# Recurrent attention and a squared-ReLU layer on one core: decays by TensorE, one written list for the first two groups, two more pieces in passes

## The chip, the cores and the metric

The kernel runs on 1 core of one Trainium2 chip. The metric is the device time of the program in microseconds (us). A core has engines that each work through their own instructions in order: TensorE (PE; its weight loads are shown as PEld), VectorE (DVE), ScalarE (ACT), GpSimd (POOL) and SyncE (SP), whose queue here issues all transfers. They wait for each other through semaphores. On-chip data lies in SBUF; TensorE writes into the eight banks of PSUM.

## The reference

Two blocks, one after the other. First a gated recurrence over 768 steps for 4 batches and 8 heads of width 48; then a layer with 2048 hidden units on the 3072 rows of 384 numbers that come out. All data of q, k, v and alpha are float32; `w_in` and `w_out` come as float64.

```python
for t in range(S):
    state = alpha[:, :, t, :, None] * state + np.einsum('bhd,bhe->bhde', k[:, :, t], v[:, :, t])
    y[:, :, t] = np.einsum('bhd,bhde->bhe', q[:, :, t], state)
...
x = attn_out.transpose(0, 2, 1, 3).reshape(B * S, H * D)
h = np.maximum(x @ w_in, 0.0)
return (h * h @ w_out)
```

## The kernel before

**Blocks.** The 768 steps are cut into 6 chunks of 128 and with 4 batches make 24 blocks of 128 rows, numbered chunk by chunk (block n is chunk n // 4 of batch n % 4). For a block, ScalarE takes logarithms of alpha (`ln`, L244), TensorE sums them along the steps with a triangular matrix (`cs`, L265 for blocks 0 to 7 in fp32, L268 and L269 after that in two parts), and ScalarE takes exponentials of the sums and of their negatives (`eb` L276, `ei` L280). VectorE multiplies q by the one and k by the other (`mq`, `mk`, L284). TensorE transposes q and k (`qT`, `kT`, L309 for blocks 0 to 3; `turn`, L482, after that, for pairs of blocks) and ScalarE or VectorE copies them out of PSUM (`qc`, `kc`, L325 and L490). Then come scores within half-blocks (`scores`, L372) and the sums of k times v (`state_sums`, L395), a masked copy of the scores (`masked`, L380), and the state: `sums_copied` (L406) and `next_state` (L420 and L421), which multiplies the new state by the decay over the whole block. Two blocks of one pair share the y products (`ga` and `gb`, L352), and `ev` (L515) copies y in twelve pieces into x, which is laid out feature by row.

**The decay over a block** is the last row of the exponentials. `bl` (L297) writes this row to DRAM, and `br` (L303) reads it back twice, element by element, so that it lies along partitions in `last`. Both go through SP's queue.

**Groups.** Four blocks, 512 rows, make a group; there are six. The layer runs group by group: 16 hidden units of 128 columns each (`ffn_in` or `in_x` with `in_y`), and then the output, four tiles of 128 rows by 384 columns, each the sum over the 16 hidden units. `w_in` and `w_out` are each cut into eight pieces of two hidden units (768 KB as float64). A piece is loaded (`load_weights`) and turned into float32 by five VectorE and two ScalarE instructions (`convert_first` L153 and L157, `convert_middle` L166 and L169, `convert_second` L175, L179, L182).

**Two kinds of products.** A plain product is fp32 (L806 for the hidden units of group one, `out_plain` for some pieces of the output). The other kind runs in three passes in the faster fp32r type: each operand is split into a high part, a rest and their difference (for w: `cast_w` L551, `rest_w` L561, `diff_w` L571; for x and the hidden values: `split_to` L597 and L598, `diff_to` L547), and three products are added (L623 for hidden units, L702 for the output, both `in_x`/`in_y` and `out_x`/`out_y`). The parts of w are also written to DRAM and read back for later groups (`keep` L556, `pump` L590). Group one uses plain products for all hidden units and for six pieces of `w_out`, and passes for the last two pieces. Group two uses passes for its hidden units, plain products for four pieces of `w_out` and passes for four (`AT['k0'] = 2`, `AT['k1'] = 4`). Groups three to six use passes throughout.

**The order of the work.** Nothing is scheduled by a compiler: each engine's order is the order in which the program calls the steps. For the first blocks it is a list of words in the code:

```python
first = """
    ln0 cs0 ei0 mk0 warm0 eb0 bl0 mq0 kT0 load0v kc0 ln1 qT0 load2a load2k cs1
    ...
    load4a kv3 am3 us3 load4k middle1 ha1 second1 ya2 yb2 ev2 weights4 first2
    ha0 hb1 middle2 hb0 st2 st3 st1
"""
```

`warm` and `zeros` in it are products whose result nobody uses (L221 and L338; `zeros` has three, on a state that holds zeros). After the list, `weave` walks through the units of TensorE's work of a group (`layer_in`, `layer_out`), adds up their costs, and puts in attention steps, conversions and splits of w when the sum reaches the time set for each (`AT`, `PLAN`, `EARLY`). A buffer that is used again makes its next writer wait for its last reader; the two alpha tiles serve blocks n % 2 (blocks 2 and 3 borrow others), and raw weight pieces have four buffers.

## Time and profile before

| | |
|---|---|
| device time, median of 3 runs | 521.2 us (520.43 to 521.31) |
| span of the profiled execution, the time of it that the page gives | 518.9 us |
| TensorE busy | 509.3 us, 98%, 5276 products |
| VectorE busy | 368.7 us, 71% |
| ScalarE busy | 299.6 us, 58% |
| transfers | 102.35 MB, mean 197 GB/s |
| chain that ended last | 93% on PE: o L702 41%, h L623 32%, h L806 7% |
| plain output products, L702 o<-w_out,hid | 160 records, 53.5 us |
| plain hidden products, L806 | 108 records, 43.7 us |
| copies of y, L515 on ACT | 132, 46.9 us |

An fp32 product shows as two records, one in passes as one for each pass. The page cuts the span into 40 slices of 13 us and shows the busy share of each engine in tenths, the clock granted to TensorE and the share of the transfer engines. Busy times are unions: overlapping instructions are not counted twice, so the mean duration of one instruction can be longer than its share of the busy time.

### The profile page before, as it was taken

The numbers are of one execution on the slowest core, as the hardware profiler recorded it, in microseconds if no ns is written. First come the engines' busy times: TensorE is split into PE (matmuls) and PEld (weight loads), VectorE is DVE, ScalarE is ACT, GpSimd is POOL, SyncE is SP. The second block draws the span as 40 slices with busy tenths as digits, with TensorE's granted clock in tenths as the row PEclk, the third lists the DMA queues.
The fourth block names the chain that finished last, engine by engine and source line by source line (L and its number), as shares of the span: only waits on it lengthen the run. The fifth ranks groups of instructions, "written<-read, shape, count | busy, mean of one in ns | idle before, by whom it ended". The sixth has DMA issues, their size and how long they took to land.

```text
span 518.9 us, 12889 instructions
## 1 busy us (share of the span) xinstructions
PE 509.3 (98%) x5276; PEld 417.9 (81%) x5276; DVE 368.7 (71%) x635; ACT 299.6 (58%) x630; POOL 5.3 (1%) x29
## 2 busy tenths in 40 slices
PE   7989999999999999999999999999999999999997
PEld 4854455668887669988899988899988899988997
DVE  4798979977978788875795576695465585364861
ACT  4668785666758554575954275954275754154620
POOL 4000000000000000000000000000000000000000
PEclk9999999999999999999999999999999999999999
DMA  9999767451879586999966787866773545898201
GB/s 160 211 267 215 206 216 239 105 170 72 265 174 223 121 303 171 290 315 209 270 145 172 257 247 193 245 156 165 241 245 124 186 120 153 273 340 294 67 0 62
DMA packets 140995, 102.35 MB, mean 197 GB/s; under 512 B 111477, under 2 KB 114569, under 8 KB 140937
## 3 DMA queue, kind: packets, MB, share of 16 engines
q1 hardware_dynamic: 140936, 101.53, 69.1%
q8 instruction: 42, 0.69, 0.5%
q14 instruction: 17, 0.13, 0.1%
HBM read 84.18 MB, written 17.33 MB: 196 GB/s over the span
## 4 chain that ended last, share of the span: by engine, by line
PE 93%; DMA 4%; DVE 1%; SPq 1%; ACT 1%; issue 0%; DVEq 0%
PE o L702 41%; PE h L623 32%; PE h L806 7%; PE y L352 4%; PE T L482 2%; PE sckv L372 2%; PE sckv L395 2%; DMA a_in<-in_alpha_dram 1%; DMA a_lent<-in_alpha_dram 1%; DMA k_in<-in_k_dram 1%; PE cs L265 1%; DMA row<-b 1%; PE cs L269 1%; DVE x L515 1%; PE cs L268 1%; SPq L109 0%
## 5 line engine op out<-in xcount | busy, mean ns | idle before, releaser
L623 PE MATMUL h<-xa,wb 128*128 128x512 f32 x240 | 68.4, 393 | 0.0
L623 PE MATMUL h<-xl,wl 128*128 128x512 f32 x240 | 67.7, 390 | 0.0
L638 ACT ACTIVATE hid<-h 128x512 f32<-128x512 f32 x40 | 23.8, 598 | 74.8 <-PE h L623 74.7
L623 PE MATMUL h<-xd,wd 128*128 128x512 f32 x240 | 66.8, 393 | 0.0
L515 ACT COPY x<-y 32x256 f32<-32x256 f32 (+2 forms) x132 | 46.9, 366 | 30.0 <-PE y L352 24.8
L702 PE MATMUL o<-wb,ha 128*128 128x384 f32 x160 | 54.5, 341 | 0.0
L702 PE MATMUL o<-wd,hd 128*128 128x384 f32 x304 | 53.7, 334 | 0.0
L702 PE MATMUL o<-w_out,hid 128*128 128x384 f32 x160 | 53.5, 490 | 0.0
L702 PE MATMUL o<-wl,hl 128*128 128x384 f32 x160 | 53.5, 335 | 0.0
L623 PEld LDWEIGHTS h<-xl,wl 128*128 128x128 f32 x240 | 45.1, 188 | 9.7
L702 PEld LDWEIGHTS o<-wd,hd 128*128 128x128 f32 x304 | 52.8, 188 | 0.0
L623 PEld LDWEIGHTS h<-xa,wb 128*128 128x128 f32 x240 | 44.5, 188 | 9.3
L623 PEld LDWEIGHTS h<-xd,wd 128*128 128x128 f32 x240 | 44.4, 188 | 9.0
L702 PE MATMUL o<-wb,hx 128*128 128x384 f32 x144 | 49.0, 340 | 0.0
L702 PE MATMUL o<-wl,hx 128*128 128x384 f32 x144 | 48.2, 334 | 0.0
L702 PEld LDWEIGHTS o<-w_out,hid 128*128 128x128 f32 x160 | 29.9, 190 | 19.7
L806 PE MATMUL h<-x,w_in 128*128 128x512 f32 (+1 forms) x108 | 43.7, 553 | 1.2 <-ACT x L515 1.2
L547 DVE TENSOR_TENSOR hid<-h,hid 128x512 f32<-128x512 f32 x40 | 27.5, 688 | 23.4 <-PE h L623 23.3
L806 PEld LDWEIGHTS h<-x,w_in 128*128 128x128 f32 x108 | 19.9, 190 | 20.9 <-issue 17.0
L597 ACT ACTIVATE ha<-hid 128x512 fp32r<-128x512 f32 x40 | 25.2, 638 | 17.2 <-DVE hl L598 10.8
L640 ACT ACTIVATE h<-h 128x512 f32<-128x512 f32 x40 | 23.3, 583 | 17.1 <-PE h L623 14.1
L547 DVE TENSOR_TENSOR osb<-o,osb 128x384 f32<-128x384 f32 x24 | 12.9, 553 | 25.8 <-PE o L702 24.6
(113 smaller groups left out, 879.5 us busy)
## 6 DMA issues: line engine op xcount, KB each, us to landing
wd<-do SPq DMA_DIRECT2D x36, 384.0 KB
wl<-lo SPq DMA_DIRECT2D x34, 384.0 KB
wl<-li SPq DMA_DIRECT2D x32, 384.0 KB
wd<-di SPq DMA_DIRECT2D x32, 384.0 KB
raw<-in_moe_w_in_dram SPq DMA_DIRECT2D x8, 768.0 KB
raw<-in_moe_w_out_dram SPq DMA_DIRECT2D x8, 768.0 KB
v_in<-in_v_dram SPq DMA_DIRECT2D x24, 192.0 KB
out_dram<-osb SPq DMA_DIRECT2D x24, 192.0 KB
```

The source lines that it names most:

```text
L352: ins = nc.tensor.matmul(out=ys[e][64 * half : 64 * half + D + G * e, m % 2, p // 2, t], lhsT=lhsT, rhs=rhs, start=(half, e) not in seen, ...
L372: nc.tensor.matmul(out=ps[e][HALF[h], 0, p, :], lhsT=ks[rows, p, HALF[h]], rhs=qs[rows, p, HALF[h]], start=True, stop=True, skip_group_che ...
L395: nc.tensor.matmul(out=ps[h][64 * e : 64 * (e + 1), 1, p, G:64], lhsT=tile_of("k", n)[HALF[h], 2 * p + e, :], rhs=tiles["v"][n % NV][HALF[ ...
L482: nc.tensor.transpose(out=ps[h][:, i, p, :], in_=rows[HALF[h], 128 * p : 128 * (p + 1)], identity=ident[HALF[h], HALF[h]],)
L515: copy(out=x[kk][to : to + m, t : t + 2], in_=blk[n]["y"][e][r : r + m, :, p // 2],)
L547: nc.vector.tensor_tensor(out=o, in0=x, in1=z, op=op)
L597: nc.scalar.activation(out=a, in_=x, func=AF.Copy, scale=NEAR * E)
L623: nc.tensor.matmul(out=acc["h", j], lhsT=here[w, "i", p][:, kk, jj * 128 : (jj + 1) * 128], rhs=x_parts[x][:, kk], start=start and kk == 0 ...
L638: nc.scalar.activation(out=hid[j], in_=x, func=AF.Copy, scale=E)
L640: nc.scalar.activation(out=x, in_=x, func=AF.Copy, scale=1.0 + E)
L702: nc.tensor.matmul(out=acc[t][:, 0:DM], lhsT=lhs[:, t * C : (t + 1) * C], rhs=rhs, start=start, stop=stop, skip_group_check=True,)
L806: nc.tensor.matmul(out=ps, lhsT=w[:, kk, c0 : c0 + 128], rhs=xT[g][kk][:, cols], start=(kk == 0), stop=(kk == KM - 1),)
```

## The change

**Decays by TensorE.** For blocks 0 to 3 the row no longer goes through DRAM. The step `dl` multiplies the logarithms with the last column of the triangular matrix, eight products of one column each, so that the sums over the block come out along partitions; `de` takes their exponentials into `last`, in two ScalarE instructions. Blocks from 4 on keep `bl` and `br`.

**One list for groups one and two.** The word list now covers everything up to the last product of group two, some 900 words, and the planner is used for groups three to six alone. The steps are finer: conversions to DRAM (`kept_l`, `kept_d`), fetches back (`fetch`), the ScalarE and VectorE halves of a split (`split_h` and `rest_h`, `split_x` and `rest_x`), each copy of y (`moved`), each half of a masked copy, transposes block by block (`turned_one`), the ReLU and the square after a hidden unit, and the scaling and adding behind products are words of their own. The hidden units of group one run in another order, and the loads of the weight pieces stand earlier in the list.

**Six pieces of group two.** Group two has plain products for two pieces of `w_out` and passes for six (`out_plain:p:t:2` and `out_x:n:t:4`). The number of plain pieces in group one stays six.

**No zero products.** The words `zeros` are gone from the order; four `warm` products remain, two at the start. All copies of y and of the transposed q and k go to ScalarE; twelve copies of y and two of the transposes were VectorE's.

```diff
-AT = {..., 'k0': 2, 'h0': 15, 'k1': 4, 'h1': 3, 'h1by': 5, ...}
+ORDER = """
+load:3:a load:0:a ln:0 warm:0 warm:0 cs:0 eb:0 ei:0 load:1:a ln:1 warm:0 load:0:k load:0:q mq:0 cs:1 ln:3 cs:3
+ei:3 eb:3 dl:3 eb:1 mk:0 ei:1 qT:0 dl:1 de:1 load:1:k mk:1 qc:0 load:1:q mq:1 qT:1 qc:1 load:2:a ln:2 kT:1
+load:3:q mq:3 kT:0 cs:2 qT:3 kc:1 load:3:k mk:3 load:1:v eb:2 ei:2 load:2:q mq:2 load:0:v sc:1 kv:1 kc:0 sc:0
+de:3 qc:3 one_masked:1:1 one_masked:1:0 us:1 kv:0 one_masked:0:0 one_masked:0:1 kT:3 kc:3 load_weights:0 dl:0
+de:0 us:0 qT:2 qc:2 sa:0 first:0 middle:0 y_states:0 y_inner:0 yb:0 moved:0:0:0 dl:2 de:2 load:2:k mk:2
+load:4:a kT:2 kc:2 warm:0 load:3:v sc:3 second:0 ln:4 kv:3 one_masked:3:0 load:2:v one_masked:3:1 us:3 sc:2
+kv:2 one_masked:2:0 moved:0:0:1 moved:0:0:2 moved:0:1:0 moved:0:1:1 moved:0:1:2 moved:0:2:0 load_weights:1
+moved:0:2:1 moved:0:2:2 moved:0:3:0 moved:0:3:1 moved:0:3:2 load:5:a cs:4 ha:1 one_masked:2:1 us:2 sa:2 eb:4
+y_states:2 first:1 load_weights:2 load_weights:3 sa:3 middle:1 y_inner:2 yb:2 ln:5 second:1 first:2 load:4:k
+moved:2:0:0 load_weights:4 moved:2:0:1 bl:4 load_weights:5 moved:2:0:2 moved:2:1:0 load:6:v moved:2:1:1
+moved:2:1:2 moved:2:2:0 moved:2:2:1 moved:2:2:2 ha:0 load:7:v moved:2:3:0 moved:2:3:1 moved:2:3:2 ei:4
+load:5:q first:3 middle:3 second:3 cs:5 eb:5 hf:2 middle:2 second:2 rf:2 ra:1 load:4:q load_weights:6 qa:1
...
+"""
...
-    for _ in range(3):
-        warm(0)
...
+    def dl(n):
+        ps = blk[n]["cs"].rearrange("a p t -> a (p t)")
+        for p in range(NP):
+            for e in range(2):
+                first = (2 * p + e) * D
+                nc.tensor.matmul(
+                    out=ps[64 * e : 64 * e + D, H * D + p : H * D + p + 1],
+                    lhsT=blk[n]["logs"][:, first : first + D], rhs=causal[:, C - 1 : C],
+                    start=True, stop=True, skip_group_check=True,
+                )
+
+    def de(n):
+        ps = blk[n]["cs"].rearrange("a p t -> a (p t)")
+        for e in range(2):
+            rows = slice(64 * e, 64 * e + D)
+            nc.scalar.activation(out=last_t[n % 4][rows], in_=ps[rows, H * D : H * D + NP], func=AF.Exp)
...
-    VECTOR = ('k0', 'q0')
+    VECTOR = AT["vec"].split()
...
-            if w == "i" or p >= NW - AT["k0"] or (x == "l" and p >= NW - AT["k1"]):
+            if w == "i" or p >= NW - 2 or (x == "l" and p >= NW - 6):
                 here[x, w, p] = t
...
+    def fetch(*key):
+        here[key] = wt("w" + key[0], FP32R, shapes[key[1]])
+        nc.sync.dma_start(out=words(here[key]), in_=kept_parts[key])
...
-    first = """
-        ln0 cs0 ei0 mk0 warm0 eb0 bl0 mq0 kT0 load0v kc0 ln1 qT0 load2a load2k cs1
...
+    for word in ORDER.split():
+        f, *given = word.split(":")
+        steps[f](*(int(x) if x.isdigit() else x for x in given))
...
-    for g in range(1, NG):
+    for g in range(2, NG):
```

More of the change, by code (lines that the diff above doesn't have):

```diff
@@ L341, in zeros @@
             )
-    SHARED = (0, 2)
     def y_begin(n):
@@ L462, in gb, with y_first, y_states @@
[L462 to L472 removed]
+    def y_first(a):
+        y_states(a)
+        y_inner(a)
+    def y_states(a):
+        product = two["y"] = y_begin(a)
+        for h in range(1 if a < B else 0, 2):
+            for m, p, e in heads(a):
+                rows = slice(64 * e, 64 * e + D)
+                s = blk[m]["u" if h else "s"]
+                product(m, p, e, s[rows, p, G * (1 - e) : 64], blk[m]["qs"][rows, p, HALF[h]], HALF[h])
@@ L499, in ev, with moved @@
+    def moved(n, p, i):
         g, t = divmod(n, GB)
-        if t == 0 and ps[0] == 0:
+        if g not in xT:
             if g == 0:
```

511 lines of the change are left out of this document (267 added, 244 removed).

## The prediction

> **What bounds the kernel now.** I read the page's slices first, then TensorE's waits, the windows by stage, the timeline of the head, and last the chain of waits.
>
> ```profile
> PE   7989999999999999999999999999999999999997
> PEclk9999999999999999999999999999999999999999
> DMA  9999767451879586999966787866773545898201
> ```
>
> TensorE is full from the third slice (13 us each) to the last, at full granted clock. The eight waits listed for it sum to 5.8 us, all before 36 us; the longest:
>
> ```profile
> PE kT L309 <- DVE k_in L284: 1.3, 1, 1.3
> PE h L806 <- ACT x L515: 1.2, 3, 0.7
> ...
> PE sckv L395 <- DMA v_in<-in_v_dram: 1.0, 2, 0.8
> ```
>
> The windows (length; busy of PE, PEld, DVE, ACT, POOL; clock; DMA share; GB/s) give what else is full:
>
> ```profile
> 0.00:13.00 13.00, 9.15 (x94) 5.89 (x94) 6.19 (x12) 5.46 (x10) 5.34 (x29) 1.00 0.99 160
> ...
> 26.00:36.00 10.00, 8.12 (x171) 5.79 (x163) 9.77 (x21) 5.33 (x12) 0.00 (x0) 1.00 1.03 246
> 36.00:52.00 16.00, 16.00 (x42) 7.80 (x42) 13.44 (x23) 14.32 (x27) 0.00 (x0) 1.00 0.98 238
> 52.00:80.00 28.00, 28.00 (x219) 13.74 (x218) 24.66 (x40) 23.11 (x42) 0.00 (x0) 1.00 0.73 211
> 80.00:127.40 47.40, 47.40 (x561) 33.12 (x560) 40.89 (x65) 30.61 (x62) 0.00 (x0) 1.00 0.48 148
> ```
>
> So the kernel has two parts: a head of 36 us, set by transfers and copies, and TensorE without a hole. Time is won by less TensorE work or by filling TensorE earlier, and lost by any new hole. From the timeline (start, length, what; in brackets the idle time before and what ended it):
>
> ```profile
> 1.10 2.93 PE L221 MATMUL warm<-s 128*128 128x256 f32 x6 [1.10 <-POOL s L67]
> ...
> 3.73 0.52 ACT L244 ACTIVATE a_in<-a_in 128x384 f32<-128x384 f32 x1 [1.72 <-DMA a_in<-in_alpha_dram]
> ...
> 16.65 0.52 ACT L244 ACTIVATE a_lent<-a_lent 128x384 f32<-128x384 f32 x1 [2.64 <-DMA a_lent<-in_alpha_dram]
> ...
> 19.63 4.05 PE L338 MATMUL zeros<-s 128*128 128x256 f32 x18
> ...
> 26.52 0.68 PE L395 MATMUL sckv<-v_in,qk_lent 64*64 64x48 f32 x32 [0.20 <-DMA v_in<-in_v_dram]
> ```
>
> The first input tile lands at 3.73, the twelfth at 16.65: 1.175 us each. The sixteenth (26.52) has two weight pieces ahead of it: (26.52 - 3.73 - 15 x 1.175) / 2 = 2.6 us a piece, decay rows included. The chain (start, length, what):
>
> ```profile
> 35.28 9.72 PE h L806 x26
> ...
> 175.56 13.10 PE o L702 x40
> ...
> 207.19 8.54 PE o L702 x48
> ...
> 515.45 0.56 DVE osb L547
> ```
>
> From 35.28 TensorE works 480.2 us to 515.45; 3.45 us of tail follow.
>
> **Six pieces in passes.** An fp32 product is two records: 40 records in 13.10 us, 0.655 us a product. Three passes: 3 x 0.175 (a run of 144 takes 25.18 us) = 0.525. Pieces 2 and 3 of group two hold 16 products: 16 x 0.13 = -2.1 us, all on the path. Added: four splits, on VectorE 4 x (0.685 + 0.692) = 5.5 us and on ScalarE 4 x 0.63 = 2.5, and two fetches of 384 KB, 1.9 us each at 206 GB/s. VectorE is busy 75.1 of the 88.3 us of group two and DMA some 0.75, so these cost nothing; uncovered, 5.5 us. The order mixes fp32 with passes: 33 changes between the kinds, 4 before. The nearest row, four passes of a sum of logs inside an fp32 run, shows none (12 records and 8 passes in 5.26 us after it, 5.33 by their rates); the other end is 18 passes after transposes, 4.33 against 4.12 after such sums: 29 x 0.2 = 6 us. I take 0. Returns from small attention products to large ones fall from 33 to 28: up to -1.0.
>
> **Zero products.** Twelve go, 5.6 us of busy time before 24 us, where TensorE waits anyway: 0, unless they keep its clock (first rival).
>
> **Decays of blocks 0 to 3.** Four row stores and eight gathers leave SP's queue; one store is on the chain at 23.61 (3.87 us). Added per block: eight one-column products, between 0.25 us (16 records at the 16 ns of the y products) and 0.65 (a whole sum of logs); I take 0.6, in a waiting TensorE; and two ScalarE exponentials, 0.25 each, below the smallest copy's 0.367. New wait: block 4's alpha reuses block 0's tile and must wait for block 0's decay products, and v of blocks 3 and 2 and w_in piece 1 stand behind it on SP. Tile 13 (v of block 0) lands at 3.73 + 12 x 1.175 = 17.8; state sums, k's transposes of block 3 and the decays take 1.5, so SP goes on at 19.3, while piece 0 and one k are still in flight to 21.6: nothing lost.
>
> **The head's new order.** ScalarE now makes all 24 copies of y (12 were VectorE's) and becomes its path. Piece 0 is behind 13 tiles: 3.73 + 12 x 1.175 + 2.6 = 20.4. Then VectorE's first step 0.48, ScalarE's two steps of piece 0 1.65, one copy 0.385 (six of them, start to next, 2.28 us; three 1.17), decay 0.5, k copy 0.48, logs 0.42, 11 copies 4.24, exponential 0.37, piece 1 1.65, logs 0.42, 12 copies 4.62: 15.2 in all, so x of group one is whole at 35.6, against 35.28 before. But TensorE has done other things by then. Before, four half-width products (0.43) and all 42 full ones (0.87) were left. Now six and 40 are left, and the sums of logs of blocks 4 and 5 (0.65 each) are done: 480.2 + 0.86 - 1.74 - 1.3 - 2.1 = 475.9.
>
> **New holes in groups one and two.** From x whole to the first product in passes, TensorE's list holds 0.87 + 13 x 2.62 full columns, 2.6 halves, 3.5 transposes, 4.3 scores and sums, 4.1 logs, 4.1 y and 17 x 1.31 out = 75.8 us. VectorE ends piece 3's conversion 3.9 us after that point (0.37 + 0.84 on ScalarE, then 2.73) and then has 12 x 2.73 + 11 x 0.94 (conversions), 6 x 0.87 (splits of w), 12 x 0.47 (q and k), 12.2 (masks, states, splits of logs and h) and 1.8 (x) = 68: done at 71.9, 3.9 us early. Nearer hand-offs, summed so: piece 2 0.8 us ahead of its first product, block 4's scores 1.0, logs of block 7 1.2, transposes 1.6 to 2.8. ScalarE loses 1.4 us waiting for piece 5's first step, so about 0.7 comes through. Bounds 0 and 6.8 (second rival). Later groups keep their order but for a few moves: 0.
>
> **Sum.** 35.6 + 475.9 + 3.45 + 0.7 = 515.7 against the span of 518.9: -3.2 us. The page gives of that execution only the span; the median of the runs, 521.2, is 2.3 above it: 518.0.
>
> **Rivals.** *The clock falls.* The first six warm-up records take 0.49 us each, zeros later 0.225: TensorE starts at half speed. Now only two warm-up products stand ahead of the first sum of logs. At half speed, what follows tile 13 (0.45 + 0.48 + 0.6 + 0.48 + 1.7 of y) ends at 25.2, not 21.5, and ScalarE wants y at 22.5: +2.7; the next y +1.7; the first full products +0.4. That ends at 522.0 (517.3 + 4.7; lists behind get that much time, so the 0.7 goes). For it: fewer fillers. Against it: at half speed the head's products up to tile 13 (4 x 1.3 logs, 2 x 1.2 decays, 5 x 0.96 transposes, 2 x 1.24 scores, 0.9 sums, 2.0 warm-up) make 17.8 of the 16.7 us there, so TensorE would be full, and it kept its clock before in windows half idle (1.00 of 2 us at 6 to 8). Chance 0.12. The Trainium skill ("TensorE: Matmul & The Clock Gate", What's actually happening) says that the clock halves after an idle window of about 3.4 us and comes back after a busy one. By that rule the scattered head could stay at half speed, which is this rival's 522.0; the trace agrees on the slow start, and its longest hole, 1.3 us, does not test the rest.
>
> *VectorE starves TensorE: slower.* The list asks 68 us of VectorE in 71.9, 95% dense. Before, over 36 to 127 us, it was busy 79.0 of 91.4, 86%. At that density the list takes 78.7 and TensorE waits 6.8 at the first product in passes: 517.3 + 6.8 = 524.1. It decides against the change below 88.5%, where the hole passes 4.9 us. For it: VectorE waited up to 2.4 us for ScalarE's conversion steps. Against it: other steps now stand between, and no VectorE step here comes more than 0.3 us ahead of ScalarE's by the sums. Chance 0.14.
>
> *The transfers are late, so the new head gives nothing.* All w_in pieces are asked for some 10 us earlier; by 54 us the queue must land 26 tiles and 8 pieces, 11.4 MB, and before it had moved 11.5 by then. For it: no slack in that. Against it: the 2.6 us a piece already holds the decay rows that go. If the first two pieces take 3.9 us each (786 KB at the 203 GB/s seen at 20 to 22 us), piece 0 is 1.3 late, and piece 7 2.6, against 1.9 in hand before its first product: 518.0 + 1.3 + 0.7 = 520.0. Chance 0.09.
>
> **How the numbers follow.** The forecast has 0.65, with a range of its own of 516 to 520. Measurement tells 0.2% (520.2 to 522.2 is no change). Low end: no hole, five cheaper returns, copies at 0.366 (-0.4): 515.3. High end 522.2 takes in the clock and the late transfers and leaves out VectorE's rival. The clock's and the transfers' 0.21 lie at the edge of that band, about half on each side: faster 0.75, same 0.11, slower 0.14.
>
> **What would show it.** Right: no wait of TensorE above 1 us after some 36 us; x of group one whole near 35.6; fp32 out records 128, not 160; 48 more records in passes, 0.175 us apart; nothing of row or last on SP before blocks 4. Wrong: warm-up-like durations (0.49) past 10 us; TensorE waiting for xl, w_in or hl on VectorE between 40 and 110 us; first conversion waiting for raw past 21 us.

## The result, and the profile after

| | before | after |
|---|---|---|
| time, median (range) | 521.04 us (520.43 to 521.31) | 528.38 us (525.93 to 529.44) |
| ratio, with its 95% interval | | 1.0136 (1.0111 to 1.0161) |
| span of the profiled execution | 518.9 us | 527.0 us |
| x of group one whole | 35.2 us | 40.2 us |
| groups three, four, five and six begin | 215.6, 294.9, 374.0, 449.2 | 219.0, 300.4, 381.4, 457.5 |

The change makes the kernel slower; the forecast was 518.0. Of the 8.1 us between the two spans, 3.4 are there when group three begins, 2.2, 1.8 and 0.9 are added by groups three, four and five, and group six adds nothing. (A group begins here with its first product of `xa` and `wb` in the timeline.) One of the runs of e15_fixed below, 532.4 us, was in a slower state of the chip, and the row of e15_fixed leaves it out.

The slices of the page, 13 us each, after the change:

```profile
PE   6989998999999999999999999999999999999997
PEclk9999999999999999999999999999999999999999
DMA  9798887493255778898876788756674444798201
```

TensorE is thinner in the first slice, and the seventh (79 to 92 us) is no longer full; the transfers are less busy in the second slice. The clock row tells of nothing. TensorE's waits show more (releaser: total, times, longest):

```profile
PE cs L349 <- ACT a_in L327: 2.5, 2, 2.0
PE h L734 <- ACT hid L771: 2.4, 3, 0.8
PE y L452 <- issue: 2.1, 4, 1.0
PE sckv L497 <- issue: 1.4, 1, 1.4
PE h L928 <- ACT x L629: 1.1, 2, 0.7
...
PE h L734 <- DMA wl<-li: 1.0, 1, 1.0
```

Before, every listed wait lay before 36 us and none was put down to "issue". Now there are three kinds behind it: "issue", where the engine waited for nothing that the profile shows; a ReLU of ScalarE (`hid`, L771), 0.8 us in each of groups three to five; and a part of w_in read back for group three (`wl`). The chain says the same in shares of the span: PE 92%, ACT 3%, DMA 2%, issue 1%.

The head in the timeline (start, length, what, and in brackets the idle time before), TensorE's, SP's and ScalarE's rows together:

```profile
5.19 1.62 PE L349 MATMUL cs<-a_in,causal 128*128 128x384 f32 x2 [2.02 <-ACT a_in L327]
...
14.38 0.49 SPq L205 DMA_DIRECT2D k_in<-in_k_dram  x1
...
19.49 1.13 PE L472 MATMUL sckv<-qs,ks 48*64 48x64 f32 x32
...
22.54 0.53 PE L383 MATMUL cs<-causal,a_in 128*48 128x1 f32 x16
...
23.16 0.37 SPq L205 DMA_DIRECT2D a_in<-in_alpha_dram  x1
...
24.17 0.94 ACT L262 ACTIVATE power<-power,rebias 128x768 uint32<-128x768 uint32 x1
...
33.82 0.63 PE L452 MATMUL y<-qs,us 48*48 48x64 f32 x28 [1.04 <-issue]
...
35.86 4.38 ACT L629 COPY x<-y 32x256 f32<-32x256 f32 x12 [1.51 <-PE y L452]
```

A sum of logs takes 1.62 us, and 32 records of scores 1.13; in the kernel before they took 0.91 and 0.69 from 12 us on. So TensorE works at half speed until some 20 us, although the clock column of this execution says 1.00 from the start: the column counts only changes that were recorded, and here the first record of a clock comes at 20.5 us. SP issues nothing between 14.9 and 23.16 (forecast: it goes on at 19.3), ScalarE's first step on a weight piece comes at 24.17 (forecast 20.9), and the last copy of y ends at 40.2 (35.6).

### The profile page after: what moved, and what is told of

Same layout as the page of the kernel before. It is cut to its first block, busy times and chain, and to the rows that moved or that the text cites. A ratio compares the mean times of both kernels' runs of the same rounds, so it can differ in the third digit from the quotient of the medians.

```text
span 527.0 us, 12977 instructions
## 1 busy us (share of the span) xinstructions
PE 510.5 (97%) x5332; PEld 422.5 (80%) x5332; DVE 364.6 (69%) x629; ACT 307.2 (58%) x656; POOL 5.3 (1%) x29
## 4 chain that ended last, share of the span: by engine, by line
PE 92%; ACT 3%; DMA 2%; issue 1%; DVE 1%; SPq 0%; POOLq 0%; DVEq 0%
PE o L831 39%; PE h L734 31%; PE h L928 8%; PE y L452 5%; PE T L588 2%; PE sckv L472 2%; ACT x L629 2%; PE sckv L497 2%; PE cs L349 1%; DMA wl<-li 1%; PE qT L410 1%; DMA a_in<-in_alpha_dram 1%; PE cs L352 1%; PE cs L353 1%; PE kT L410 0%
## 5 line engine op out<-in xcount | busy, mean ns | idle before, releaser
L831 PE MATMUL o<-wb,ha 128*128 128x384 f32 x168 | 59.1, 352 | 0.0
L629 ACT COPY x<-y 32x256 f32<-32x256 f32 (+1 forms) x144 | 50.5, 364 | 13.6 <-PE y L452 11.5
L831 PE MATMUL o<-wd,hd 128*128 128x384 f32 x320 | 56.4, 334 | 0.0
L831 PE MATMUL o<-wl,hl 128*128 128x384 f32 x168 | 56.2, 335 | 0.0
L831 PEld LDWEIGHTS o<-wd,hd 128*128 128x128 f32 x320 | 55.6, 188 | 0.0
L831 PE MATMUL o<-wb,hx 128*128 128x384 f32 x152 | 51.2, 337 | 0.0
L831 PE MATMUL o<-wl,hx 128*128 128x384 f32 x152 | 50.8, 334 | 0.0
L831 PE MATMUL o<-w_out,hid 128*128 128x384 f32 x128 | 44.8, 489 | 0.0
L831 PEld LDWEIGHTS o<-w_out,hid 128*128 128x128 f32 x128 | 23.8, 189 | 12.9
L831 PEld LDWEIGHTS o<-wb,ha 128*128 128x128 f32 x168 | 31.5, 188 | 1.5
```

The costliest lines, as they stand in the source:

```text
L629: copy(out=xT[g][kk].rearrange("a (t c) -> a t c", c=C)[to : to + m, t : t + 2], in_=blk[n]["y"][e][r : r + m, :, p // 2],)
L831: nc.tensor.matmul(out=acc[t][:, 0:DM], lhsT=lhs[:, t * C : (t + 1) * C], rhs=rhs, start=start, stop=stop, skip_group_check=True,)
```

## The experiments

Where the runs stand, in one table. "x" is the time at which x of group one is whole; "rest" is the span less the start of group two, for the kernels made from before, in which nothing behind the head was changed; "records" is how many product records more than in before TensorE has behind it when group two begins; "issue" is the sum of the holes put down to issue after x is whole; cells of a column that does not apply are empty. x, records, issue and rest are of the one profiled execution. The head of after, e2 and e6 is the same list of words, and x is 40.2, 39.5 and 38.3 there, so among the kernels made from after a difference of 2 us in x says nothing by itself.

| run | made from | time (range) | ratio (95%) | x | records | issue | rest |
|---|---|---|---|---|---|---|---|
| before | | 521.0 | | 35.2 | 0 | 0 | 391.6 |
| after | | 528.4 | 1.0136 | 40.2 | | 2.45 | |
| e1_warm | after | 529.5 (529.2 to 530.2) | 1.0156 (1.0141 to 1.0171) | 40.6 | | 3.0 | |
| e2_whole | after | 526.2 (525.6 to 527.8) | 1.0095 (1.0075 to 1.0116) | 39.5 | | 3.4 | |
| e3_both | after | 528.2 (526.2 to 528.5) | 1.0121 (1.0099 to 1.0143) | 40.4 | | 3.3 | |
| e4_before_cold | before | 522.0 (521.1 to 522.4) | 1.0006 (0.9997 to 1.0016) | 35.8 | -4 | 0 | 391.5 |
| e5_before_nozeros | before | 524.2 (524.0 to 524.8) | 1.0065 (1.0050 to 1.0080) | 36.1 | -24 | 1.8 | 393.9 |
| e6_spread | after | 526.6 (525.8 to 527.5) | 1.0115 (1.0098 to 1.0132) | 38.3 | | 0.9 | |
| e7_unblock | after | 530.1 (529.6 to 534.1) | 1.0196 (1.0159 to 1.0233) | 41.6 | | 1.6 | |
| e8_before_six | before | 536.3 (534.7 to 536.9) | 1.0291 (1.0274 to 1.0308) | 35.8 | | 0 | |
| e9_before_decays | before | 527.3 (524.9 to 529.9) | 1.0123 (1.0088 to 1.0159) | 35.4 | +64 | 3.2 | 394.0 |
| e10_all | after | 528.1 (526.6 to 531.3) | 1.0150 (1.0113 to 1.0186) | 44.8 | | 1.1 | |
| e11_shift64 | before | 529.1 (527.7 to 531.0) | 1.0162 (1.0138 to 1.0186) | 42.2 | +64 | 1.5 | 393.5 |
| e12_shift128 | before | 530.7 (530.3 to 530.9) | 1.0190 (1.0173 to 1.0207) | 45.3 | +128 | 0 | 391.5 |
| e13_decays_slot60 | before | 526.0 (523.8 to 526.1) | 1.0085 (1.0064 to 1.0105) | 40.0 | +124 | 0.4 | 392.1 |
| e14_before_slot60 | before | 525.2 (523.7 to 525.8) | 1.0075 (1.0058 to 1.0092) | 39.3 | +60 | 0.5 | 392.1 |
| e15_fixed | after | 527.5 (522.8 to 528.6) | 1.0098 (1.0064 to 1.0132) | 43.9 | | 0 | |
| e16_decays_piece | before | 525.7 (525.1 to 525.9) | 1.0086 (1.0066 to 1.0107) | 39.1 | +124 | 0 | 391.5 |
| e17_before_piece | before | 524.9 (524.3 to 525.5) | 1.0070 (1.0051 to 1.0090) | 37.9 | +60 | 0.5 | 392.1 |
| e18_filled | after | 526.3 (524.4 to 527.8) | 1.0095 (1.0062 to 1.0129) | 40.5 | | 1.0 | |

**First: the clock, and the later groups.** The first theory was the rival of the prediction, the clock; the second loss in sight was that of groups three to six.

```diff
 e1_warm:  -load:3:a load:0:a ln:0 warm:0 warm:0 cs:0
           +load:3:a load:0:a ln:0 warm:0 warm:0 warm:0 warm:0 cs:0
 e2_whole: the planner's units of groups three to six as in the kernel before
           (in_x with in_scaled, out_x for four tiles and so on as one unit)
 e3_both:  both
 e4_before_cold (of before):
           -    for _ in range(3):
           +    for _ in range(1):
                    warm(0)
```

> The changed kernel with four warm-up products ahead of the first sum of logs instead of two; nothing else. Theory of the clock: TensorE ran at half speed until 20.5 us of the changed kernel (a sum of logs 1.49 to 1.65 us for two records, 0.81 later) because two warm-up products were too short a burst; with four, as in the kernel before, it is at full speed from about 4 to 5 us, ScalarE's conversion of w_in piece 0 starts near 21 us instead of 24.2, x of group one is whole 3 to 4 us earlier than 40.2, and the span falls from 527.0 to some 523.3. Rival: the head is held by SP, which stood from 14.9 to 23.2 us behind block 0's decay products, and by late transfers; then TensorE is fast but x is whole no earlier than 39 us and the span stays at 526 to 527.

> The changed kernel, but the planner of groups three to six gets its units whole again (the products of a hidden unit with their scaling, a pair of output products with all four tiles, ReLU with square), so that every engine's order in these groups is that of the kernel before; groups one and two as changed. Theory of the finer units: the 4.8 us that groups three to five lost (81.5, 80.9 and 76.1 us against 79.3, 79.2 and 75.2) come from ScalarE freeing a bank of PSUM behind copies of y, so they go, and the span falls from 527.0 to 522.2, the clock's loss in the head staying. Rival: the holes there come from transfers or from the state that group two leaves behind (a fetch of w_in's rest was waited for at 223 us); then groups three to five stay above 80, 80 and 76 us and the span at 525 or more.

> Both of the two edits: four warm-up products, and whole units in groups three to six. If the two causes are separate the gains add: 527.0 - 3.7 - 4.8 = 518.5 of span, about 520.3 of device time, a little faster than the kernel before (521.0). If the earlier head only moves the holes of groups one and two (2.3 us of issue holes and 1.4 us of slower products there), the sum is not reached: 520 to 522 of span.

> The kernel before with one warm-up product at its start instead of three; the zero products stay. Theory of the clock: the first burst ends before 2.2 us and TensorE waits for the first alpha until 4.3, so it stays at half speed (kT and qT of block 0 at 1.1 us for four records instead of 0.65) until the head is busy for some microseconds on end, at the zero products at the latest; the head is 1 to 4 us later and the span 520 to 523. Rival: the fillers do nothing for the clock, or the head has slack for a slow TensorE: the span stays at 518.9 within 0.5.

The clock theory falls as a theory of the clock alone. With two more warm-up products (e1) sums of logs take 0.9 us from 8 us on, yet x is whole no earlier, as the rival had it (its span of 526 to 527 was missed by 1 us), for now TensorE stands in the head where it had not:

```profile
18.55 0.53 PE L383 MATMUL cs<-causal,a_in 128*48 128x1 f32 x16
22.01 1.01 PE L410 MATMUL qT<-ident,qk_lent 128*128 128x128 f32 x4 [2.94 <-issue]
```

Behind this hole four transposes take 1.0 us, not 0.6, and 32 records of scores 1.13 up to 30 us: TensorE is back at half speed for some 10 us. In the kernel before, a clock that comes at 7.9 us and not at 4.3 costs at most 0.6 us of the head (e4: x at 35.8, time within 0.2%, at the edge of its rival's span); a head at half speed to 20 us was not tried there. Both edits together (e3) gave 528.2 with a span of 526.4; the forecasts were spans of 518.5 and of 520 to 522.

Whole units give 2.2 us by the medians, 528.4 to 526.2, though the two intervals of the ratio overlap a little. In the profiled executions the gain is smaller: groups three to five take 82.1, 80.5 and 75.2 us, 237.8 together against 238.5 in the changed kernel and 233.6 before, so by groups three and four and by the span (526.0) the run looks like its rival, and group five alone is that of before. TensorE's waits of that run (total, times, longest) have one wait for the ReLU left of three:

```profile
PE y L452 <- issue: 2.5, 4, 1.1
PE h L734 <- DMA wl<-li: 1.6, 1, 1.6
...
PE h L734 <- ACT hid L771: 0.8, 1, 0.8
```

Of the three waits the two of groups four and five went with the undoing; the one of group three stayed. The two are gone in all five kernels with whole units (e2, e3, e10, e15, e18) and there in all four with the finer ones (after, e1, e6, e7): that the finer units bring them is shown. How they do it is not. ScalarE does not come later to this ReLU: here are the same place of group three in the kernel before and in the changed kernel, TensorE's and ScalarE's rows.

```profile
240.42 1.13 ACT L515 COPY x<-y 32x256 f32<-32x256 f32 x3 [0.69 <-PE y L352]
241.22 0.97 PE L623 MATMUL h<-xa,wb 128*128 128x512 f32 x3
241.46 0.59 ACT L657 ACTIVATE hid<-h 128x512 f32<-128x512 f32 x1
...
245.09 1.13 ACT L629 COPY x<-y 32x256 f32<-32x256 f32 x3 [0.69 <-PE y L452]
246.13 0.59 ACT L771 ACTIVATE hid<-h 128x512 f32<-128x512 f32 x1
246.77 0.98 PE L734 MATMUL h<-xa,wb 128*128 128x512 f32 x3 [0.80 <-ACT hid L771]
```

In both, three copies of y stand ahead of the ReLU. Before, TensorE begins the next hidden unit 0.8 us ahead of the ReLU's end; after the change it waits for that end. In group three of e2 all 103 instructions of ScalarE stand in the order of the kernel before, and the wait is there all the same. So the changed kernel's next hidden unit needs something that this ReLU frees, and that of the kernel before did not; that this is the PSUM bank, given out in the order in which the program calls the steps, is argued, for the profile does not name banks. The wait for `wl` is not touched by it; it is there in every run made from after (0.7 to 1.6 us) and in none made from before.

**Second: what "issue" is.** All holes of this kind follow one pattern. The trace has, beside the program's transfers, a queue that brings instructions (q8 on the page: 42 packets, 0.69 MB, so 16.4 KB each, one for 127 of the 5332 product records). The stretch ahead of the hole at 89.53, in the changed kernel's timeline:

```profile
83.71 0.69 PE L472 MATMUL sckv<-qs,ks 48*64 48x64 f32 x32
84.33 0.46 PE L588 MATMUL T<-ident,k_in 64*128 64x64 f32 x8
...
84.98 0.69 PE L452 MATMUL y<-qs,s 48*48 48x64 f32 x32
...
87.38 0.63 PE L452 MATMUL y<-am,v_in 64*48 64x64 f32 x31
87.80 0.38 PE L497 MATMUL sckv<-v_in,k_in 64*64 64x48 f32 x11
89.53 0.55 PE L497 MATMUL sckv<-v_in,k_in 64*64 64x48 f32 x21 [1.35 <-issue]
90.02 1.24 PE L831 MATMUL o<-w_out,hid 128*128 128x384 f32 x3
```

The view of the transfers in the window from 86.8 to 88.1 has one packet of that queue:

```profile
q8 instruction: 1, 0.02, 5.4%
```

TensorE stops in the middle of 32 equal products on data that has long been there. The packets against the holes, in us:

```
                     packet starts  lands    hole ends   after landing
after                 31.55        32.43     33.82       1.39
                      86.90        88.03     89.53       1.50
                     167.47       168.45    169.93       1.48
                     180.46       181.51    183.02       1.51
                     317.46       318.87    320.24       1.37
before, no zeros     235.26       236.69    238.10       1.41
before, decays       100.86       101.82    103.20       1.38
                     265.58       266.55    268.06       1.51
                     315.36       316.80    318.30       1.50
```

A hole ends 1.4 to 1.5 us after a packet has landed, 2.3 to 2.9 us after it was started. And holes lie at fixed places in the stream: counted in TensorE's records, those of the changed kernel come after 473, 1103, 1863, 2117 and 3632 records. The distances, 630, 760, 254 and 1515, are 5, 6, 2 and 12 times 126 to 127. In e2 and e7 the holes come at the same counts, in e1, with two products more at its start, at counts one lower (1102, 1862, 2116): the bound stays in the stream while the work moves on by four records. I read this so: TensorE's instructions come in pieces of 16 KB with fixed bounds, and it stands at a bound when it has run through the records ahead faster than the next piece comes. Small attention products take 16 ns a record; large ones 175 to 330. Run time alone does not decide, though. Counted on from the holes, the piece of the changed kernel that ends near the 4517th record is run through in 2.2 us and there is no hole; its packet was started 1.3 us before TensorE began that piece. The piece ahead of the hole at 33.82 took 5.3 us; its packet was started 4.0 us after TensorE had begun it. Ahead of more than half of the holes behind the head it is 0.5 to 1.3 us after. What sets the start of a packet is not shown.

Two runs go at the change's side of this, one by moving products and one by taking SP's stand away:

```diff
 e6_spread (of after): three words moved
   hf:13            to ahead of  kv:6
   out_plain:0:0:2  to ahead of  sc:10
   out_plain:0:1:2  to ahead of  y_states:10
 e7_unblock (of after): three words moved
   load:3:v load:2:v load_weights:1   to ahead of  load:4:a
```

> The changed kernel with three large products moved in the written list: one full hidden unit of group one (2.6 us) to between the inner y products and the state sums of block 6, and two plain output steps of group two (1.3 us each) to between the runs of small attention products that end at 170 and 184 us. Theory one (TensorE's instructions do not come fast enough for more than some 160 small products in a row): the holes of 1.35, 0.50 and 0.44 us before 'issue' shrink to under 0.3 in all, group three starts 2 us earlier (217.0, not 218.98), time 526.3. Theory two (these holes are set by something the products wait for): they stay within 0.3 us of their size, time 528.4.

> The changed kernel with v of blocks 3 and 2 and the second piece of w_in issued ahead of block 4's alpha, so that SP no longer stands from 14.9 to 23.2 us with transfers behind it that need not wait for block 0's decay products. Theory one (the standing SP is what makes the head late): the DMA share of 20 to 24 us rises from near 0 to over 0.8, x of group one is whole 2 to 4 us earlier than 40.2, time 524.5 to 526.5. Theory two (TensorE at half clock and ScalarE's order set the head): x whole within 1 us of 40.2, time 527.5 to 529.

In e6 the holes at 89.5, 169.9 and 183 are gone; one of 0.88 us is new at 83.2, one piece earlier in the stream (976 records), in a run of small products that the moved hidden unit no longer parts from those ahead. Group three begins at 216.3, and the time is 1.8 lower, with intervals that overlap. Of the 2.7 us by which group three is earlier, 2.0 lie ahead of x, where nothing was changed: in this execution TensorE came to full speed at 11 us and, but for 3.4 us, stayed there. The first theory is borne out for the places that were mended, not for the time; the new hole was not foreseen. In e7 SP issues through (the DMA share of 20 to 24 us is 1.03, against 0.01), and x is whole later, not earlier: y of block 2 is stopped by a hole of 1.86 at 34.80, which the changed kernel had at the same records with 1.04. Neither theory's time fits, and what a free SP is worth could not be told apart from the holes.

**Third: the parts of the change one by one, in the kernel before.**

```diff
 e5_before_nozeros: the words zeros2 (four times) taken out of the list
 e8_before_six:     -'k1': 4     +'k1': 6
 e9_before_decays:  -bl0 ... br0 ... bl1 ... br1 ... (blocks 0 to 3)
                    +dl0 de0 ... dl1 de1 ...
```

> The kernel before without its twelve zero products in the head, nothing else changed. Theory one (the zero products do nothing but fill a TensorE that waits): 521.0, within 0.5. Theory two (they keep TensorE's clock up between 14 and 24 us; without them the granted clock falls to half there as it does in the changed kernel, where x of group one comes 5.0 us later): x of group one whole 1.5 to 3 us later than 35.2, a time of 522.5 to 524.

> The kernel before with six pieces of group two's w_out in passes, not four, by the planner and its times as they are; nothing else. Theory one (the price of the prediction, 16 products at 0.13 us less, and nothing else): 518.9. Theory two (the parts of six pieces keep their buffers to the end of group two, so that the first parts of w_in for group three are fetched late): TensorE waits 1 to 1.6 us for wl at the start of group three, time 520 to 521.

> The kernel before with the decays of blocks 0 to 3 summed by TensorE and their exponentials by ScalarE in place of the rows through DRAM; list otherwise as it was, zero products kept. Theory one (the forecast's step: 0.6 us a block in a waiting TensorE and two exponentials of 0.25 us): 521.0, within 0.5. Theory two (12 transfers less on SP's queue bring the late tiles of the head forward): x of group one 0.5 to 1.0 earlier, 520.0 to 520.5. Theory three (the one-column products and what waits for them stretch the head): x of group one 1 to 2.4 us later, 522 to 523.4.

Without zero products the windows of the head (length; busy of PE, PEld, DVE, ACT, POOL; clock; DMA share; GB/s) show what they were for:

```profile
15.00:20.00 5.00, 3.69 (x90) 2.50 (x90) 2.86 (x8) 2.06 (x5) 0.00 (x0) 1.00 0.75 183
20.00:25.00 5.00, 1.80 (x8) 1.43 (x8) 4.42 (x10) 4.58 (x10) 0.00 (x0) 0.78 0.87 215
25.00:30.00 5.00, 5.00 (x134) 4.58 (x133) 4.58 (x11) 2.26 (x4) 0.00 (x0) 0.54 1.09 273
```

The clock falls: TensorE waits 3.4 us in one piece for VectorE, and is at half speed for 0.22 x 2 x 5 + 0.46 x 2 x 5 = 6.8 us. The Trainium skill ("TensorE: Matmul & The Clock Gate", What's actually happening) gives a window of about 3.4 us after which an idle TensorE halves its clock; the trace agrees with the length, 6.8 being two such windows, but a window wholly without work was not needed: in e3 the clock is at half from 12.9 us on, and the longest hole of the 6 us before is 1.0 us. x is only 0.9 us later by it, less than the second theory's 1.5 to 3, and the time a little above its 522.5 to 524. The larger part of the 3.2 us comes in group three, which nobody touched:

```profile
PE kT L309 <- DVE qk_lent L284: 3.4, 1, 3.4
PE y L352 <- issue: 2.0, 2, 1.8
```

Twelve products fewer are 24 records fewer; the bounds of the pieces fall elsewhere, and one of them, at 238.1, into a run of small products.

The decays alone have the same signature. The head is as before (x at 35.4, clock full), and then come 64 records more. TensorE's waits (total, times, longest), and the place in group one:

```profile
PE o L720 <- issue: 1.6, 1, 1.6
PE y L370 <- issue: 1.6, 2, 1.3
```

```profile
101.22 0.66 PE L370 MATMUL y<-am,v_in 64*48 64x64 f32 x28
103.20 0.33 PE L370 MATMUL y<-am,v_in 64*48 64x64 f32 x3 [1.31 <-issue]
103.46 2.85 PE L720 MATMUL o<-w_out,hid 128*128 128x384 f32 x8
```

In the kernel before the same products run through, since the bound lies elsewhere. None of the three theories had this. The forecast's price of the decays themselves stands, their effect on the stream was missing in it.

Six pieces by the planner's old times are a failure of another kind, 15 us, and no measure of the written list: in group two TensorE waits for VectorE,

```profile
PE cs L268 <- DVE hi L256: 4.1, 1, 4.1
PE o L702 <- DVE osb L738: 3.9, 1, 3.9
PE o L702 <- DVE hl L598: 2.1, 2, 1.6
```

and the clock falls with it (0.95 from 128 to 230 us). VectorE itself waits 7.0 us there for decay rows on SP's queue. The expected late `wl` did not show.

**Fourth: is it the place of the bounds?** If it is, a shift by 64 records should make holes in the kernel before and one by 128 should not. Two fillers were tried ahead of the first sum of logs, then two in the head's slot of zero products, without and with the decays (64 records).

```diff
 e11_shift64, e12_shift128 (of before): the third warm-up product replaced by
+    for i in range(33):        # 65 in e12
+        nc.tensor.matmul(out=tiny[0:D, i : i + 1], lhsT=s_t[0][:, 0, 0:D], rhs=s_t[0][:, 0, 0:1], ...)
 e14_before_slot60, e13_decays_slot60 (of before, of e9):
-   zeros2 zeros2 zeros2 kc2
+   tiny2 tiny2 tiny2 kc2       # each 13 products of 128 rows and one column
 e17_before_piece, e16_decays_piece (of before, of e9):
-   zeros2 zeros2 zeros2 kc2
+   zeros2 tiny2 zeros2 kc2     # 33 products of 48 rows, 48 and 64 columns
```

> The kernel before with its third warm-up product replaced by 33 products of one column, 66 records for 2, so that everything behind stands 64 records further on in TensorE's stream of instructions; no other work or order changes. Theory one (TensorE's instructions come in pieces of 128 product records, and it stands where a piece is needed within some 2.5 us of being asked for, so that it matters where the pieces begin): the order of before with the pieces begun half a piece off has 1 to 4 holes before 'issue' of 0.3 to 1.8 us after 36 us, in places where the work is that of before; 523 to 526. Theory two (the holes belong to the new order of work, and before has none by its order): no hole, 521 to 522.

> As the one with 64 records, but with 65 one-column products, so that everything stands 128 records further on, one whole piece. Theory one: the pieces begin at the same work as in before, no hole over 0.2 us after 36 us, 521 to 522, and 2 us or more under the run with 64. Theory two (more small products in the head cost time in themselves, or no hole in either): equal to the run with 64 or slower by up to 1 us.

> The kernel before with the decays by TensorE (64 records more, which alone gave 527.25), and in the head, where TensorE waits, three of its four words of zero products replaced by 13 one-column products each, 78 records for 18. Behind the head everything now stands 124 records further on than in before, almost one whole piece of 128. Theory one (where the pieces of 128 records begin decides, and the decays cost nothing in themselves): no hole before 'issue' over 0.2 us after 36 us, the time back to 520.5 to 521.5, 6 us under the decays alone. Theory two (the decays cost the time, by the head or by later clashes): 526 or more, for nothing of them is taken away.

> The kernel before with that replacement alone: no decays by TensorE, everything behind the head 60 records further on, half a piece. Theory one: holes before 'issue' near 103 and 266 us (0.5 to 1.6 each) and perhaps near 316 and 395, where a piece is then run through in under 2 to 2.6 us; 523 to 527, the head as in before to within 0.5. Theory two: no holes, 521.

> The kernel before with the decays by TensorE, all zero products but three kept, and in place of those three (6 records, 1.35 us of a waiting TensorE) 33 products of 48 rows, 48 and 64 columns (66 records, some 1.06 us at the 16 ns of the y products): 124 records more than before in all, almost one whole piece, and the clock kept by the nine large zero products that stay. Theory one (pieces and clock decide): clock full from 5 us on, x of group one whole at 35.2 to 36, no hole before 'issue' over 0.3 us, time 520.8 to 522. Theory two (the decays cost time in themselves): 525 or more.

> The kernel before with that replacement alone, 60 records more, about half a piece. Theory one: holes before 'issue' of 1 to 3.5 us in all after 36 us, near 102, 265, 315 or 395, though nothing there was changed; time 522.5 to 525, and above the run with the decays as well. Theory two: 521, no holes, below the run with the decays.

As times four of theory one's six missed, and the two that fit (e14, e17) fit for another reason: every filler made the head longer. By the times alone theory two has e13 and e16 right (526.0 and 525.7, against 526 and 525 or more), and e17 came out below e16 and not above it: with a filler in the head the decays cost 0.7 to 0.8 us of time, and x is 0.8 to 1.2 us later in those runs. Theory two fails where the decays are absent, in e11, e14 and e17, which are not at 521. The one-column products took 81 ns a record at the start (130 in 10.56 us), those of 48 columns 59 (66 in 3.88), not the 16 they were put down for; and the one-column ones did not keep the clock (behind them TensorE is at half speed for some 10 us, in e13 and e14 alike).

What the fillers were for can still be read, from behind the head, where all these kernels do the work of before. The table's last column: with 0, 124 (e16) and 128 records more it is 391.5 to 391.6 us; with 60 or 64 it is 392.1 to 394.0, and e13, the other one of 124, has 392.1 (a hole of 0.4 at 239.9; its packet was started some 2 us after TensorE had begun the piece, in e16 ahead of that, and why is not shown). In e11 1.4 of the 393.5 is a wait for VectorE at 250.8, not a hole of this kind; its largest one, 1.1, is in group one. The windows by group of e16, which has the decays, from 40 us on:

```profile
40.00:131.80 91.80, 91.80 (x821) 55.01 (x820) 78.91 (x125) 68.04 (x128) 0.00 (x0) 1.00 0.58 164
131.80:220.00 88.20, 88.20 (x1055) 70.59 (x1054) 75.11 (x134) 54.01 (x120) 0.00 (x0) 1.00 0.75 206
220.00:299.30 79.30, 79.30 (x921) 71.35 (x920) 54.26 (x100) 45.50 (x103) 0.00 (x0) 1.00 0.81 238
```

and those of e9, the decays without the filler:

```profile
40.00:129.10 89.10, 87.79 (x807) 52.50 (x806) 75.30 (x117) 64.43 (x121) 0.00 (x0) 1.00 0.59 168
129.10:217.20 88.10, 88.10 (x1054) 70.56 (x1053) 75.15 (x134) 54.01 (x120) 0.00 (x0) 1.00 0.76 211
217.20:298.40 81.20, 79.53 (x922) 71.41 (x921) 54.49 (x100) 45.50 (x103) 0.00 (x0) 1.00 0.78 227
```

The first two numbers of a row are length and busy time of TensorE. With a whole piece more TensorE is full; with half a piece it is 1.3 and 1.7 us short, on the same work but for some records in the first row. So the holes of the decays are a matter of where the bounds fall. With 60 records (e14, e17) the holes were 0.2 to 0.3 us where 64 (e9) gave 1.3 to 1.6. For the one near 105 us the count says why: it comes behind two records of the large product that follows the small ones, no longer ahead of it, and so the piece ahead is run through in 2.9 us and not in 2.1. For the others the size is not explained.

**Last: can the changed kernel be mended?**

```diff
 e10_all (of after):  e2_whole + e6_spread + e7_unblock
 e15_fixed (of after): e2_whole + e6_spread, and for blocks 0, 1 and 3
-   dl:n ... de:n          +   bl:n ... br:n      (48 records fewer)
 e18_filled: e15_fixed and
+   warm:0 warm:0 ahead of cs:0; zeros:0 ahead of qT:1; zeros:0 ahead of y_inner:0
```

> The changed kernel with three edits at once: SP unblocked, the three large products moved between runs of small ones, and the units of groups three to six whole as before. If the losses are separate, the gains add: 2.2 (whole units) + 1.8 (spread) + what the unblocked SP gives (0 to 3): 521.5 to 524.5. If the holes for want of instructions only move with every shift of the stream, 524.5 to 527, with at least two holes over 0.4 us before 'issue' after 36 us at places where none were.

> The changed kernel with the three large products moved, whole units in groups three to six, and the decays of blocks 0, 1 and 3 by rows through DRAM again (block 2 keeps TensorE's): 48 records fewer, by which no piece of 128 behind the head is run through in under 2.9 us, and block 4's alpha no longer waits for TensorE. Theory one: no hole before 'issue' over 0.3 us after 36 us, and at most one in the head; TensorE's two holes of groups three to six left (0.9 for wl, 0.8 for hid): from 526.6 by -2.2 (whole units) and -2 (holes) to 522.4, less what the head gains. Theory two (the gains do not add, as when SP was unblocked and all three edits were made): 526 to 528.

> The changed kernel as in the run with all mended (large products moved, whole units, rows for the decays of blocks 0, 1 and 3), and with large products back in its head: two more warm-up products at the start, three zero products before q of block 1 is transposed and three between the two parts of y of block 0. Theory one (the head is late because the clock falls and because small products stand without large ones): clock full from 7 us with no fall, x of group one whole 3 us or more earlier than 42.9 us, time 522 to 524.5. Theory two (the head's order itself, ScalarE's copies, is late): x whole after 40, 526 or more.

The gains do not add: e10 misses both times. e15, at 527.5, is in the range of its second theory. In it no hole of issue is left behind the head, as the count of records had it; but there are two in the head, 3.6 us in all, x is whole at 43.9, and the runs scatter from 522.8 to 528.6. In e18 TensorE is at full speed from 7 us to 31, without a hole of issue in the head, and x is whole at 40.5 all the same, as its second theory had it. ScalarE's rows of e18 in the head:

```profile
24.16 0.94 ACT L261 ACTIVATE power<-power,rebias 128x768 uint32<-128x768 uint32 x1 [3.33 <-DVE power L248]
...
36.10 4.38 ACT L628 COPY x<-y 32x256 f32<-32x256 f32 x12 [1.86 <-PE y L451]
```

It waits for VectorE's first step on weight piece 0, which had to wait 3.0 us for the piece (four reads of decay rows stand ahead of it on SP, 2.3 us), and for y of block 2. No version made here beats the kernel before.

## Why the prediction was wrong

The forecast had group three begin at 35.6 + 475.9 + 0.7 - 299.9 = 212.3 (the last number is what the kernel before takes from there to TensorE's end); it began at 219.0. TensorE ended at 523.6, not 512.2: 11.4 us between forecast and run, by step:

- **"The head's new order", x whole at 35.6: failed, +4.6.** Measured 40.2. Its sums took TensorE at full speed and "SP goes on at 19.3, nothing lost": TensorE was at half speed to 20.5, the sums of logs 1.6 us and not 0.91, and SP went on at 23.2. The rival *the clock falls* names this and its price, 4.7; at 0.12 its chance was set too low, on the reasoning that TensorE would be full at half speed. That its price comes so near the 4.6 is luck: 1.0 of the 4.6 is a hole of issue ahead of y of block 2, which the rival does not have. And the runs do not leave the clock as the sole cause: where it was mended (e1, e18) another wait took its place, and with SP issuing through (e7) x came no earlier either. How the 4.6 divides among clock, SP and holes stays open.
- **"Returns from small attention products to large ones fall from 33 to 28: up to -1.0", and "New holes in groups one and two", 0.7: failed, 2.3 us of other holes (89.5, 169.9, 183.0).** Attention products were put closer together and this was counted as a gain. It is what runs a piece of the instruction stream through faster than the next one comes. The holes that were looked for, hand-offs from VectorE, are not there: TensorE waits for VectorE nowhere behind 36 us, so the rival *VectorE starves TensorE* was rightly held unlikely in the written list, though it is what happened to six pieces under the planner's old times.
- **"Later groups keep their order but for a few moves: 0": failed, +4.8.** In them are 2.4 us of waits for the ReLU, 1.0 for `wl` and 0.2 of issue as listed. Laid against the same products of the kernel before, from start to start, these places cost 2.6, 1.2 and 0.7 us (one of issue, at 349.6, is too short to be listed), 4.5 of the 4.8. Whole units take away two of the three waits for the ReLU (e2). The finer units were seen, and not followed to what each hidden unit then waits for.
- **"Two fetches ... cost nothing": failed by the 1.0 for `wl`** at the start of group three. The first three parts of this kind are asked for 5.5, 1.5 and 0.1 us ahead of group three, in the kernel before 8.6, 3.9 and 2.5. That six pieces keep their buffers longer would do it; this is argued, not shown, and e8, which has six pieces too, has no such wait.
- **"Zero products", "0, unless they keep its clock": failed, +3.2 in the kernel before (e5).** There they do keep the clock, and with it 0.9 us of the head. Most of the rest is the hole at 238, which their 24 records had kept away.
- **"Decays of blocks 0 to 3", with nothing for them in the sum: held for the operations and failed for the kernel.** 0.53 us a block at full speed and 0.81 at half, against 0.6; x as before in e9. But alone they are 6.2 us slower by the median; the profiled execution, the fastest of the four, is 4.2 us longer than that of before, 3.2 of it listed as holes of issue. With the filler of e16 the work behind the head takes 391.5 us, that of before.
- **"Six pieces in passes", -2.1, with nothing for the changes between kinds: held as far as it can be seen.** Head and holes explain 6.2 of the 6.7 us by which group three is late; what is left, 0.4, is all that the other terms can have missed by together, though they may offset each other. The plain output records are 128, as said. Alone it was not measured.

The sign was wrong because three losses that the sum had at 0 to 0.7, each of 2 to 5 us, stood against a gain of 3.2. That the kernel before had no hole at all should have been read as a narrow state: by the count of records the quickest piece behind its head is run through in some 2.8 us, and 24 records fewer (e5) or 64 more (e9) bring pieces of 2.1.

Three slips in its working change nothing in this. The third slice of TensorE's row reads 8, and TensorE is full from 36 us on, as the windows say. The clock rival's three terms add up to 4.8. The low end's three terms give 518.0 - 0.7 - 1.0 - 0.4 = 515.9, not 515.3.

## What to carry to other kernels

Where many small products follow each other, look at the queue that brings instructions and count records: in these runs about every second piece of 126 to 127 records that was run through in 2 to 3 us behind the head had a hole at its end, and so had a slower one whose packet started late. So put a large product into every such run, and expect that adding or removing a few products early moves holes into parts that nobody touched. Judge a "useless" filler by the clock of the window behind it and by its records before taking it out. When a planner's units are made finer, compare every wait of the groups that it plans with those of before, for the buffers may then be given out in another order.

## What the runs showed of the hardware that was not expected

- TensorE's instructions come in pieces of 16.4 KB, one for 126 to 127 product records; in these runs a stand for them ends 1.2 to 1.6 us after the piece has landed (1.4 to 1.5 in most), and such a piece takes 0.9 to 1.5 us to land.
- From 1.5 us into such a stand of 2.9 us, in the head of e1, TensorE was at half speed for some 10 us. Spells at half speed elsewhere were 6.8 us (e5) and, by a clock column of 0.72 over 30 to 36 us, 3.4 (e18).
- Small products are not cheap in every shape: 16 ns a record for the y products (48 rows, 48 and 64 columns), 59 for fillers of the same shape that all write one place, 50 for 128 rows and one column at full speed (29 in 1.46 us), 81 at half.
- Fillers of one column kept TensorE busy for 3.9 us and the clock still fell (e14: transposes 0.60 us ahead of them, 1.12 behind); zero products of 256 columns in the same slot kept it.
